# Loading the second token tile of x from ScalarE's queue, and splitting its transposes over four banks, at the start of a SwiGLU feed-forward kernel

## The chip, the core and the metric

The kernel runs on one core of one Trainium2 chip. The metric is the device time of one execution in microseconds (us); lower is better.

## The reference

The function is a SwiGLU feed-forward layer in bf16, with 2048 tokens, model width D = 512 and hidden width F = 1376:

```
B, S, D, F = 1, 2048, 512, 1376
g = _silu(x @ w_gate)
u = x @ w_up
return (g * u) @ w_down
```

## The kernel before

**Tiling.** Tokens are worked in four chunks of 512 (`SC`), hidden features in ten full tiles of 128 and a remainder of 96, and the model width in four slices of 128 (`KD`). TensorE sums over the partition dimension, so both gate and up products need x with its width on the partitions: that is `xT_sb`. A product for one chunk and one feature tile (a "G" group for the gate, a "U" group for up) is four matmuls, one for each width slice, into one PSUM bank. ScalarE applies silu to the G bank, VectorE multiplies the result with the U bank and writes the hidden tile `hT_sb`. The remainder has groups of its own (X and Y). At the end sixteen token tiles ("O" groups) are multiplied with `w_down`, copied out of PSUM and stored.

**Engines and order.** Each engine has its instructions written out in order; they meet through semaphores. The planner lists the groups in the order in which TensorE works them; group number n uses bank n modulo 8 (`NB`), and TensorE takes a bank again after the readers of the group eight places earlier are done (`free`, from the third G or U group on).

**The start.** This is where the change lies. TensorE first runs six matmuls on constants (`N_WARM`, line 290). The first 256 tokens of x come in as they lie in memory, as two token tiles of 128 by 512 (`x0_sb`, loads named t0 and t1, line 101, issued by SyncE). TensorE transposes them by multiplying with an identity (line 297), in four "T" groups: each holds two 128 by 128 transposes in one bank and is copied into `xT_sb` by one copy of 256 columns. The first two width slices of each tile are copied by ScalarE (line 235), the last two by VectorE (line 246). Tokens 256 to 511 come through a transposing load (named x0b, line 76) straight into `xT_sb`.

The first G and the first U group are worked in halves (line 282): G on tokens 0 to 255, U on tokens 0 to 255, then G and U on tokens 256 to 511. In the first halves, the matmul on slice dk waits for the copies that hold slices up to dk; these copies are listed in `x0_ready` with their first slice, engine and place. The second halves wait for x0b. All later groups take 512 tokens at once.

**Loads.** The weights come in slabs of feature tiles, a gate slab and an up slab each: tile 0, tile 1, tiles 2 and 3, tiles 4 to 6, and the rest. In the text wg0 and wu0 are the gate and up slabs of tile 0, wg1 and wu1 those of tile 1, wg2 and wu2 those of tiles 2 and 3. ScalarE issues wg0 and wu0 (line 81), then runs a small silu on constants, ahead of which its function table is loaded (line 224). SyncE issues, in this order, t0, t1, x0b, then wg1, wu1, wg2, wu2 and the rest, the other three chunks of x by transposing loads, and `w_down`.

Of the kernel before, what the change touches and what calls it, by code (L numbers as in the profile page):

```python
# [12 lines left out]
def bass_standalone__swiglu_ffn__prompt_kernel(nc, x, w_gate, w_up, w_down, out):  # L13
    _, S, D = x.shape
    F = w_gate.shape[1]
    P = 128
    KD = D // P
# [5 lines left out]
    TPC = SC // P  # L23
# [8 lines left out]
    xf = x[0]  # L32
# [8 lines left out]
    with ExitStack() as es:  # L41
# [4 lines left out]
        xT_sb = sb("xT_sb", [P, KD, S], BF16)  # L46
# [7 lines left out]
        x0_sb = sb("x0_sb", [P, TPC // 2, D], BF16)  # L54
# [11 lines left out]
        def load_sem(name):  # L66
            loads[name] = sem(f"s_{name}")
            return loads[name]
# [6 lines left out]
        def load_x(eng, name, t0, t1):  # L75
            eng.dma_start_transpose(
                xT_sb[:, :, t0:t1], xf[t0:t1, :]
            ).then_inc(load_sem(name), 16)

        def load_w(eng, name, src, base, f0, f1):  # L80
            eng.dma_start(
                w_sb[:, :, base + f0:base + f1],
                src[:, f0:f1].rearrange("(k p) f -> p k f", p=P),
            ).then_inc(load_sem(name), 16)
# [4 lines left out]
        def load_gate(eng, a, b):  # L89
            load_w(eng, f"wg{a}", w_gate, 0, a * P, min(b * P, F))  # L90

        def load_up(eng, a, b):
            load_w(eng, f"wu{a}", w_up, UPH, a * P, min(b * P, F - 32))

        def loads_on_scalar(act):
            load_gate(act, *slabs[0])
            load_up(act, *slabs[0])

        def loads_on_sync(sp):
            for t in range(TPC // 2):  # L100
                sp.dma_start(x0_sb[:, t, :], xf[t * P:(t + 1) * P, :]).then_inc(load_sem(f"t{t}"), 16)
            load_x(sp, "x0b", HT, SC)
            for a, b in slabs[1:]:
                load_gate(sp, a, b)
                load_up(sp, a, b)
            load_w(sp, "wut", w_up, F - (F - 32), F - 32, F)
            for c in range(1, NSC):
                load_x(sp, f"x{c}", c * SC, (c + 1) * SC)
            sp.dma_start(
                wd_sb[:, 0:NFF, :], w_down[0:NFF * P, :].rearrange("(k p) d -> p k d", p=P)  # L110
            ).then_inc(load_sem("wd"), 16)
            sp.dma_start(wd_sb[0:F_LAST, NFF, :], w_down[NFF * P:F, :]).then_inc(load_sem("wdt"), 16)
# [7 lines left out]
        def add_group(kind, **what):  # L120
            g = dict(kind=kind, at=len(groups), bank=banks[len(groups) % NB], readers=[], **what)
            groups.append(g)
            return g

        def add_op(eng, g, **what):
            n_read[eng] += 1
            op = dict(g=g, at=n_read[eng], **what)
            (act_ops if eng == "A" else dve_ops).append(op)
            g["readers"].append((eng, op["at"]))
            return op  # L130
# [46 lines left out]


        x0_ready = []
        for t in range(TPC // 2):  # L180
            for half, eng in enumerate("AD"):
                g = add_group("T", t=t, k0=2 * half)
                op = add_op(
                    eng, g, kind="copy", stored=(s_I, 0),
                    out=xT_sb[:, 2 * half:2 * half + 2, t * P:(t + 1) * P],
                    src=g["bank"][:, 0:2 * P].rearrange("p (k t) -> p k t", k=2),
                )
                x0_ready.append((2 * half, eng, op["at"]))
        n_T = len(groups)

        for c in range(NSC):
# [7 lines left out]
        for t in range(NST):  # L199
# [3 lines left out]
            for c0, c1 in halves:  # L203
                g = add_group("O", t=t, c0=c0, c1=c1)
                eng = "A" if len(halves) == 2 and c0 == 0 else "D"
                op = add_op(
                    eng, g, kind="copy", out=o_sb[ob][:, c0:c1], src=g["bank"][:, 0:c1 - c0],
                    stored=(s_out[ob], need),
                )
# [4 lines left out]
        def on_sync(sp):  # L214
            loads_on_sync(sp)
            for t, c0, c1, ob, eng, n in stores:
                sp.wait_ge(s_A if eng == "A" else s_D, n)
                sp.dma_start(of[t * P:(t + 1) * P, c0:c1], o_sb[ob][:, c0:c1]).then_inc(s_out[ob], 16)
            for i in range(NOS):
                sp.wait_ge(s_out[i], 16 * n_store[i])  # L220

        def on_scalar(act):
            loads_on_scalar(act)
            act.activation(adummy[:, 0:4], zero_c, ACT.Silu)  # L224
            for op in act_ops:
                act.wait_ge(s_P, op["g"]["at"] + 1)
                if op["kind"] == "silu":
                    if op["free"]:
                        act.wait_ge(s_D, op["free"])
                    fn = ACT.Silu  # L230
                else:
                    if op["stored"][1]:
                        act.wait_ge(*op["stored"])
                    fn = ACT.Copy
                act.activation(op["out"], op["src"], fn).then_inc(s_A, 1)  # L235
# [13 lines left out]
        def on_tensor(pe):  # L249
            landed = set()  # L250

            def need(name):
                if name not in landed:
                    pe.wait_ge(loads[name], 16)
                    landed.add(name)
# [36 lines left out]
            pe.wait_ge(s_I, 1)  # L292
            for g in groups[:n_T]:
                need(f"t{g['t']}")
                for i in range(2):
                    k = g["k0"] + i
                    ins = pe.matmul(  # L297
                        g["bank"][:, i * P:(i + 1) * P], lhsT=x0_sb[:, g["t"], k * P:(k + 1) * P],
                        rhs=ident[:, :], start=True, stop=True,
                    )  # L300
                ins.then_inc(s_P, 1)
# [4 lines left out]
            for g in groups[n_T + 2:]:  # L306
# [27 lines left out]
                else:  # L334
                    t, c0, c1 = g["t"], g["c0"], g["c1"]
# [18 lines left out]
        on_sync(nc.sync)  # L354
        on_scalar(nc.scalar)
        on_tensor(nc.tensor)
        on_vector(nc.vector)

# [27 lines left out]
```

## Time and profile before

| | |
|---|---|
| time, median of 3 runs | 121.23 us (120.81 to 121.36) |
| the profiled execution | 121.29 us, of which the span from first to last instruction is 120.0 us |
| TensorE matmul | 117.0 us busy, 97% of the span |
| VectorE, ScalarE | 44.5 us (37%), 31.1 us (26%) |
| data moved | 8.51 MB, nearly all of the loads in the first fifth of the span |

PE is TensorE's matmuls, PEld its weight loads, DVE VectorE, ACT ScalarE, POOL GpSimd, SP SyncE; a "q" behind an engine's name is its sequencer, which issues the DMAs. Times in the profile count from the first instruction of the program. A duration of a matmul runs from its start to its modelled end; since matmuls overlap, the distance from start to start is what one costs.

### The profile page before, as it was taken

What the parts mean: (1) busy time and instruction counts of PE and PEld (TensorE: products, weight loads), DVE (VectorE), ACT (ScalarE), POOL (GpSimd) and SP (SyncE); (2) the same over time, 40 slices, a digit from 0 to 9 for tenths busy, and PEclk for the clock granted to TensorE, in tenths of its full rate; (3) what the DMA queues carried; (4) which work ended last, traced back from release to release, by engine and by line L of the source; (5) the groups of instructions that cost most, each with busy time, mean ns of one, the idle gap of its engine ahead of it and who ended that gap; (6) DMA issues with size and microseconds to landing.
All of it is one profiled execution on the core that took longest, in us unless ns stands there. A gap on an engine that the chain in (4) does not pass through costs nothing.

```text
span 120.0 us, 1415 instructions
## 1 busy us (share of the span) xinstructions
PE 117.0 (97%) x561; PEld 53.9 (45%) x561; DVE 44.5 (37%) x66; ACT 31.1 (26%) x53; POOL 0.5 (0%) x5
## 2 busy tenths in 40 slices
PE   7899999999999999999999999999999999999993
PEld 2564444444444444444444444344444444444452
DVE  0224433444434444334444334466233224222420
ACT  3333233262333272333262333230000000000001
POOL 1000000000000000000000000000000000000000
DMA  3999999930000000000000000000211121111112
GB/s 89 231 306 372 287 218 182 302 127 0 0 0 0 0 0 5 0 0 5 0 0 0 0 5 0 0 0 0 87 44 44 52 85 44 44 66 66 44 44 87
DMA packets 17254, 8.51 MB, mean 71 GB/s; under 512 B 10496, under 2 KB 17248, under 8 KB 17248
## 3 DMA queue, kind: packets, MB, share of 16 engines
q1 hardware_dynamic: 16192, 8.16, 25.4%
q10 hardware_dynamic: 1056, 0.26, 1.0%
q8 instruction: 4, 0.07, 0.3%
q14 instruction: 2, 0.02, 0.0%
HBM read 4.49 MB, written 2.10 MB: 55 GB/s over the span
## 4 chain that ended last, share of the span: by engine, by line
PE 97%; ACT 0%; DVE 0%; issue 0%
PE bank L282 58%; PE bank L344 32%; PE bank L316 3%; PE bank L290 2%; PE bank L327 2%; PE bank L297 1%; ACT xT_sb L235 0%; DVE o_sb L246 0%
## 5 line engine op out<-in xcount | busy, mean ns | idle before, releaser
L282 PE MATMUL bank<-xT_sb,w_sb 128*128 128x512 bf16 (+1 forms) x328 | 70.2, 376 | 0.4 <-ACT xT_sb L235 0.4
L282 PEld LDWEIGHTS bank<-xT_sb,w_sb 128*128 128x128 bf16 x328 | 32.2, 98 | 37.7 <-issue 0.6
L242 DVE TENSOR_TENSOR hT_sb<-sg_sb,bank 128x512 bf16<-128x512 f32 x40 | 27.5, 688 | 40.8 <-PE bank L282 37.6
L344 PE MATMUL bank<-wd_sb,hT_sb 128*128 128x512 bf16 (+4 forms) x187 | 38.3, 367 | 0.0
L235 ACT ACTIVATE sg_sb<-bank 128x512 f32<-128x512 f32 x40 | 23.8, 596 | 41.6 <-PE bank L282 41.6
L344 PEld LDWEIGHTS bank<-wd_sb,hT_sb 128*128 128x128 bf16 (+1 forms) x187 | 17.8, 98 | 20.7 <-DVE hT_sb L242 0.4
L246 DVE CAST o_sb<-bank 128x512 bf16<-128x512 f32 (+1 forms) x16 | 10.7, 667 | 25.4 <-PE bank L344 25.3
L235 ACT ACTIVATE o_sb<-bank 128x384 bf16<-128x384 f32 x1 | 0.5, 490 | 38.2 <-PE bank L344 38.2
L316 PE MATMUL bank<-xT_sb,w_sb 128*128 128x512 bf16 x16 | 4.1, 379 | 0.0
L242 DVE TENSOR_TENSOR hT_sb<-sgx_sb,bank 32x512 bf16<-32x512 f32 x4 | 2.8, 692 | 3.5 <-ACT sgx_sb L235 3.5
L290 PE MATMUL bank<-const-bfloat16-1.0 128*128 128x512 bf16 x6 | 2.7, 623 | 0.8 <-PEq L371 0.8
L235 ACT ACTIVATE sgx_sb<-bank 32x512 f32<-32x512 f32 x4 | 2.3, 587 | 4.5 <-PE bank L316 4.5
L242 DVE TENSOR_TENSOR hT_sb<-sgy_sb,bank 64x512 bf16<-64x512 f32 x4 | 2.7, 685 | 0.1
L316 PEld LDWEIGHTS bank<-xT_sb,w_sb 128*128 128x128 bf16 x16 | 1.6, 98 | 1.9
L246 DVE CAST xT_sb<-bank 128x256 bf16<-128x256 f32 x2 | 0.8, 424 | 4.2 <-PE bank L297 4.0
L235 ACT ACTIVATE sgy_sb<-bank 64x512 f32<-64x512 f32 x4 | 2.4, 589 | 0.1
L327 PE MATMUL bank<-xT_sb,w_sb 128*64 128x512 bf16 x16 | 1.9, 382 | 0.0
L224 ACT ACT_TABLE_LOAD x1 | 1.3, 1283 | 1.9 <-issue 1.9
L290 PEld LDWEIGHTS bank<-const-bfloat16-1.0 128*128 128x128 bf16 x6 | 0.7, 133 | 1.9 <-issue 1.9
L327 PEld LDWEIGHTS bank<-xT_sb,w_sb 128*64 128x64 bf16 x16 | 0.8, 109 | 1.0 <-DVE hT_sb L242 0.4
L297 PE MATMUL bank<-ident,x_sb 128*128 128x128 bf16 x8 | 1.2, 309 | 0.0
L297 PEld LDWEIGHTS bank<-ident,x_sb 128*128 128x128 bf16 x8 | 0.8, 133 | 0.8 <-issue 0.5
(7 smaller groups left out, 1.7 us busy)
## 6 DMA issues: line engine op xcount, KB each, us to landing
out_dram<-o_sb SPq DMA_DIRECT2D x15, 128.0 KB, 1.7
wd_sb<-in_w_down_dram SPq DMA_DIRECT2D x1, 1280.0 KB, 6.9
w_sb<-in_w_gate_dram SPq DMA_DIRECT2D x1, 480.0 KB, 5.5
w_sb<-in_w_up_dram SPq DMA_DIRECT2D x1, 448.0 KB, 6.1
w_sb<-in_w_gate_dram SPq DMA_DIRECT2D x1, 384.0 KB, 4.6
w_sb<-in_w_up_dram SPq DMA_DIRECT2D x1, 384.0 KB, 5.1
x_sb<-in_x_dram SPq DMA_DIRECT2D x2, 128.0 KB, 2.5
w_sb<-in_w_gate_dram SPq DMA_DIRECT2D x1, 256.0 KB, 3.9
```

The source lines that it names most:

```text
L224: act.activation(adummy[:, 0:4], zero_c, ACT.Silu)
L235: act.activation(op["out"], op["src"], fn).then_inc(s_A, 1)
L242: ins = dve.tensor_tensor(op["out"], op["a"], op["b"], ALU.mult)
L246: ins = dve.tensor_copy(op["out"], op["src"])
L282: ins = pe.matmul(g["bank"][:, n0:n1], lhsT=w_sb[:, dk, col:col + P], rhs=xT_sb[:, dk, c * SC + n0:c * SC + n1], start=(dk == 0), stop=(dk ...
L290: pe.matmul(banks[NB - 1][:, :], lhsT=ones_w, rhs=ones_m, start=True, stop=True)
L297: ins = pe.matmul(g["bank"][:, i * P:(i + 1) * P], lhsT=x0_sb[:, g["t"], k * P:(k + 1) * P], rhs=ident[:, :], start=True, stop=True,)
L316: ins = pe.matmul(g["bank"][:, :], lhsT=w_sb[:, dk, XC0:XC0 + P], rhs=xT_sb[:, dk, c * SC:(c + 1) * SC], start=(dk == 0), stop=(dk == KD - 1),
L327: ins = pe.matmul(g["bank"][y0:y1, :], lhsT=w_sb[:, dk, YC0:YC0 + 64], rhs=xT_sb[:, dk, c * SC:(c + 1) * SC], start=(dk == 0), stop=(dk == ...
L344: ins = pe.matmul(g["bank"][:, 0:c1 - c0], lhsT=hT_sb[0:K, fk, t * P:(t + 1) * P], rhs=wd_sb[0:K, fk, c0:c1], start=(fk == 0), stop=(fk == ...
```

## The change

The load of token tile 1 goes from SyncE to ScalarE, as ScalarE's first load, ahead of wg0 and wu0. So the transposing load x0b becomes SyncE's second load. Tile 0 keeps its two T groups of two transposes each; tile 1 gets four T groups of one transpose each, whose copies of 128 columns go to ScalarE and VectorE in turn (slices 0 and 2 to ScalarE, 1 and 3 to VectorE). There are six T groups in place of four, so every later group has a bank two places on.

```diff
+        def load_t(eng, t):
+            eng.dma_start(x0_sb[:, t, :], xf[t * P:(t + 1) * P, :]).then_inc(load_sem(f"t{t}"), 16)
+
         def loads_on_scalar(act):
+            load_t(act, 1)
             load_gate(act, *slabs[0])
             load_up(act, *slabs[0])
 
         def loads_on_sync(sp):
-            for t in range(TPC // 2):
-                sp.dma_start(x0_sb[:, t, :], xf[t * P:(t + 1) * P, :]).then_inc(load_sem(f"t{t}"), 16)
+            load_t(sp, 0)
             load_x(sp, "x0b", HT, SC)
...
         x0_ready = []
-        for t in range(TPC // 2):
-            for half, eng in enumerate("AD"):
-                g = add_group("T", t=t, k0=2 * half)
+        for t, nk in ((0, 2), (1, 1)):
+            for k0 in range(0, KD, nk):
+                eng = "AD"[(k0 // nk) % 2]
+                g = add_group("T", t=t, k0=k0, nk=nk)
                 op = add_op(
                     eng, g, kind="copy", stored=(s_I, 0),
-                    out=xT_sb[:, 2 * half:2 * half + 2, t * P:(t + 1) * P],
-                    src=g["bank"][:, 0:2 * P].rearrange("p (k t) -> p k t", k=2),
+                    out=xT_sb[:, k0:k0 + nk, t * P:(t + 1) * P],
+                    src=g["bank"][:, 0:nk * P].rearrange("p (k t) -> p k t", k=nk),
                 )
-                x0_ready.append((2 * half, eng, op["at"]))
+                x0_ready.append((k0, eng, op["at"]))
...
             for g in groups[:n_T]:
                 need(f"t{g['t']}")
-                for i in range(2):
+                for i in range(g["nk"]):
```

## Prediction

> **What bounds the kernel now.** I read the chain of waits first, to see whether anything but TensorE sets the end.
>
> ```profile
> 0.84 2.72 PE bank L290 x6
> 3.56 0.80 PE bank L297 x6
> 4.36 0.02 issue
> 4.38 0.39 ACT xT_sb L235
> 4.77 0.14 issue
> 4.91 17.95 PE bank L282 x88
> ```
>
> From 4.91 us on the chain is TensorE without a break up to the last copy; nothing after that is touched by the change except bank numbers, which keep their distance of eight. So all that can be won lies ahead of 4.91, plus what a late load can add shortly behind it. The last link before the G group is ScalarE's copy of tile 1, with 0.14 us from its end to the first G matmul.
>
> Next the timeline of 3.3 to 5.0 us, for what that copy waited for.
>
> ```profile
> 3.81 0.38 ACT L235 ACTIVATE xT_sb<-bank 128x256 bf16<-128x256 f32 x1 [0.45 <-PE bank L297]
> 3.94 0.34 PEld L297 LDWEIGHTS bank<-ident,x_sb 128*128 128x128 bf16 x4 [0.23 <-DMA x_sb<-in_x_dram]
> 4.02 1.00 DVE L246 CAST xT_sb<-bank 128x256 bf16<-128x256 f32 x2 [4.02 <-PE bank L297]
> 4.38 0.38 ACT L235 ACTIVATE xT_sb<-bank 128x256 bf16<-128x256 f32 x1 [0.19 <-PE bank L297]
> ```
>
> TensorE waited 0.23 us for t1 (it landed at 3.90), ScalarE then 0.19 us for tile 1's transposes. The copies are short, but the two engines have two each, in a row.
>
> Then the busy time by stretches, for TensorE's speed and the load on the DMA engines:
>
> ```profile
> core 0: us, PE busy (x) PEld busy (x) DVE busy (x) ACT busy (x) POOL busy (x), PEclk, DMA share, GB/s
> 2.00:3.00 1.00, 1.00 (x4) 0.29 (x2) 0.00 (x0) 1.00 (x1) 0.00 (x0) 1.00 0.93 250
> 5.00:6.00 1.00, 1.00 (x6) 0.63 (x6) 0.02 (x1) 0.00 (x0) 0.00 (x0) 1.00 1.09 194
> 6.00:7.00 1.00, 1.00 (x11) 0.90 (x10) 0.00 (x0) 0.09 (x1) 0.00 (x0) 1.00 0.94 214
> ```
>
> All matmuls in the last two rows have 256 columns at most, and the count nearly doubles. In the records of single matmuls the start-to-start distance of the 256-column matmuls is 0.213 us up to 5.92 and 0.109 us from 6.06 on; the one between, 0.133, puts the switch to the full rate at about 5.98. (The PEclk column shows 1.00 throughout; the distances do not.) By 5.98 the G/U work has done 5.25 matmuls. The DMA engines are full from 2.0 us on, so a load that goes sooner pushes another back.
>
> Last, the issue-to-landing times of the loads:
>
> ```profile
> x_sb<-in_x_dram SPq DMA_DIRECT2D x2, 128.0 KB, 2.5
> w_sb<-in_w_gate_dram ACTq DMA_DIRECT2D x1, 128.0 KB, 2.7
> w_sb<-in_w_up_dram ACTq DMA_DIRECT2D x1, 128.0 KB, 3.6
> xT_sb<-in_x_dram SPq DMA_TRANSPOSE x1, 4.1
> ```
>
> With the issue times this gives landings at 3.07 (t0), 3.52 (wg0), 3.90 (t1), 4.94 (wu0), 5.84 (x0b), then 6.39, 7.39 and 8.14 (wg1, wu1, wg2). They follow one another; no two land together.
>
> **The change, part by part.** *The issues.* ScalarE's queue gets one more issue, 0.40 us by SP's rows for t0 and t1 (0.398 and 0.411), plus some 0.03 of gap. wg0 is issued at 1.23 instead of 0.80, wu0 at 1.73 instead of 1.29. Behind them the table load (1.28 us) starts at 2.29 instead of 1.85, and the small silu (0.20) ends at 3.79 instead of 3.35. ScalarE's first copy started at 3.81 after a wait of 0.45: this wait is the cover, and it is used up to 0.02 us. If ScalarE's issues take 0.53 each, as its second did, the first copy is some 0.1 late. SyncE loses one issue: x0b and all its later loads are issued 0.46 earlier, which wins nothing by itself as the DMA engines are full.
>
> *t1's landing.* Not in the trace from ScalarE's queue. Best case: as t0, issue plus 2.27, 3.07. Worst: where t1 lands now, 3.90. I take wg0's row, the first load of that queue: issue plus 2.7, 3.5. Needed at about 3.75, so TensorE's wait for t1 goes, and its eight transposes run from 3.35 to 4.20 at 0.107 each, instead of to 4.35.
>
> *The copies.* ScalarE's 256- and 512-column operations take 383 and 597 ns, so 128 columns take about 276 (an estimate on the same line); VectorE's 424 and 667 give 303. Each engine has one copy of 256 and two of 128: ScalarE 0.94 us instead of 0.77, VectorE 1.03 instead of 0.85. That is 0.17 to 0.18 more work each, on the path, against finer waits. From ScalarE's first copy (3.81 to 4.19): slice 0 of tile 1 is ready at 4.49, slice 2 at 4.80. VectorE (first copy 4.02 to 4.45): slice 1 at 4.78, slice 3 at 5.11. Each start of a matmul comes 0.145 after the copy it waits for, as now (4.761 to 4.906). So G on slice 0 starts at 4.64, on slice 1 at max(4.64 + 0.213, 4.78 + 0.145) = 4.93, slice 2 at 5.14, slice 3 at 5.35 (5.11 + 0.145 is sooner), and U at 5.56. Before, U started at 5.71. The two added waits of TensorE have only the four G matmuls behind them. Gain: 0.15 us at the slow rate.
>
> *What that is worth.* If the switch to the full rate stays at 5.98, the 0.15 us holds 0.7 of a slow matmul, which would have cost 0.109 each later: 0.07 to 0.08 us. If the switch moves with the start, 0.15. I take 0.10.
>
> The Trainium skill has a rule that bears on this, "TensorE: Matmul & The Clock Gate", Part 1 (The HAM clock gate): the full clock comes after about 3.4 us of a free-running window with enough activity, so an earlier start would only move work into the slow time. By that rule the sum would be the 0.07; no row of one profile shows whether the switch is tied to the clock or to the work.
>
> *The loads behind.* wg0 now is second on its queue. If it takes t1's present place, it lands at 3.90; needed at 4.6, cover 0.7. wu0, third, between its present 4.94 and x0b's 5.84 (by then all five first loads are through whatever their order); needed at 5.45, which is 0.11 ahead of its matmul. I take 5.2, nearer to the present row, since x0b's transfer cannot start before its own issue of 1.3 us is well under way (now 3.81 in the packet records, 2.08 after its issue began; by that 3.35 after the change). x0b stays at about 5.84, needed at 6.1 instead of 6.28: cover 0.2. wg1, wu1, wg2 have 0.66, 0.52 and 0.63 us to their matmuls (by the single records), more than the 0.15 that TensorE gains. All this hides.
>
> A second rule speaks against the change: "DMA: Bandwidth & Descriptors", section "Issuing engines are not separate DMA queues", says that loads from several engines run on the same 16 DMA engines and interleave, so a second queue only saves issue time. By it t1's gain is taken from t0 and wg0; this is the first rival below, with the landings above as its measure.
>
> **Sum.** 121.29 (profiled) - 0.10 = 121.19. The profiled execution lies 0.06 above the median of the runs: 121.1.
>
> **The rivals.** *t0 is passed by t1.* The two equal loads are issued within 0.01 us of each other, and t0 has no head start any more. Landings are 0.38 to 0.44 apart now; if t1 goes first, t0 lands at about 3.47, and the transposes start at 3.62 instead of 3.35. Everything up to U moves by 0.27: U at 5.83, 0.12 later than now, 0.06 us lost in all: 121.3. For it: the same engines, equal shapes. Against it: in the present profile SP's load did land first though both queues started together.
>
> *The full rate comes sooner,* since TensorE's pause at 3.8 for t1 goes. At most all eight first-half matmuls run at 0.109, but x0b, at 5.84, then holds the second halves until about 5.98 instead of 6.28: 0.30 gained, 120.9. Beyond this the weights would bind: wu1 allows 0.52. So no case on these rows gains much over 0.5 us, and a clear gain of over 0.6 is nearly shut out.
>
> *Slower: wu0 lands late.* It is third on ScalarE's queue, and shares the DMA engines with x0b's and then wg1's packets, which now start sooner. From a landing of 5.6 on U starts later than now. At x0b's row (5.84) U starts at 5.95, which costs 0.14 to 0.24. If it is pushed to where wg1 lands now, 6.39, U starts at 6.5; 1.25 matmuls that were done by 5.98 come at the full rate after it: 0.52 + 0.14 = 0.66, 121.9. Against it: the two queues' packets alternate about evenly when both are waiting (packet records, 3.0 to 3.3 us), and wu0 has half of x0b's bytes.
>
> **How the numbers follow.** 0.5% is 0.6 us, about what a measurement of this kernel can tell from no change (three runs spread over 0.55). Forecast: 0.50 (121.0 to 121.3). t0 passed: 0.18. Sooner full rate: 0.12. wu0 late: 0.15, of it 0.1 far enough to cost over 0.6. The last 0.05 is a later full rate after new pauses of TensorE, which would cost half of the delay. Faster by over 0.5%: 0.12, from runs that come out low in the first and third case; within: 0.66; slower: 0.22, the late wu0, the late full rate and runs that come out high. The range takes the first three cases with 0.3 us of spread of the runs on both sides, and half of the fourth: 120.5 to 121.8.
>
> **What would show it.** Right: t1 lands before 3.75 and no PEld wait on x_sb between the transposes; ScalarE's 128-column copies at 0.28 us; the first G matmul at 4.6 to 4.7, and U at 5.5 to 5.6; the chain of waits unbroken after it. Wrong: the first transpose later than 3.4 (t0 passed); a PE wait on a w_sb or xT_sb load behind 4.6 us (a load late); the 0.109 distance starting far from 5.98; or any difference after 24 us.

## The result, and the profile after

The changed kernel takes 121.84 us (median of ten runs, 121.49 to 123.57); the kernel before, run beside it, 121.16 (120.81 to 121.62). The ratio is 1.0047, with a 95% interval of 1.0029 to 1.0066: slower by about half a per cent. Two of the ten runs came in a slower state (123.42 and 123.57) and are left out of the ratio. The profiled execution took 121.81 us, its span is 120.5 instead of 120.0.

The chain of waits of the changed kernel (start, length, what):

```profile
1.71 0.03 issue
1.74 4.57 DMA w_sb<-in_w_up_dram
6.31 0.05 issue
6.35 17.02 PE bank L286 x84
23.38 0.86 PE bank L320 x4
24.24 17.27 PE bank L286 x80
```

Where ScalarE's copy of tile 1 stood, there is a load: wu0, issued at 1.74 and landed at 6.31. The chain is unbroken from 6.35 on, and from here it runs 0.52 us behind the kernel before (second chunk at 24.24 instead of 23.72). So the whole loss is made before 6.35.

The timeline from 3.3 us on:

```profile
3.55 0.78 PEld L301 LDWEIGHTS bank<-ident,x_sb 128*128 128x128 bf16 x8 [0.90 <-issue]
3.58 1.01 PE L301 MATMUL bank<-ident,x_sb 128*128 128x128 bf16 x8
3.99 0.81 ACT L239 ACTIVATE xT_sb<-bank 128x256 bf16<-128x256 f32 x3 [0.20 <-PE bank L301]
4.20 0.82 DVE L250 CAST xT_sb<-bank 128x256 bf16<-128x256 f32 x3 [4.20 <-PE bank L301]
4.73 0.65 PE L286 MATMUL bank<-xT_sb,w_sb 128*128 128x256 bf16 x4
6.35 1.38 PE L286 MATMUL bank<-xT_sb,w_sb 128*128 128x256 bf16 x11 [0.97 <-DMA w_sb<-in_w_up_dram]
```

The pause between the transposes of tile 0 and tile 1 is gone (eight in one piece), but they start at 3.58 instead of 3.35. G still starts sooner, at 4.73 instead of 4.91. Then four matmuls, and an idle time of 0.97 us before U.

The busy time by stretches:

```profile
5.00:6.00 1.00, 0.38 (x4) 0.10 (x1) 0.02 (x1) 0.00 (x0) 0.00 (x0) 1.00 1.33 248
6.00:7.00 1.00, 0.65 (x6) 0.59 (x7) 0.00 (x0) 0.00 (x0) 0.00 (x0) 1.00 1.18 308
```

TensorE is idle for most of a microsecond while the DMA engines move more than they did in this stretch before (248 GB/s against 194): not too few bytes, but other ones than those it waits for.

The issues, with the time to landing last:

```profile
x_sb<-in_x_dram ACTq DMA_DIRECT2D x1, 128.0 KB, 2.8
x_sb<-in_x_dram SPq DMA_DIRECT2D x1, 128.0 KB, 2.6
w_sb<-in_w_gate_dram ACTq DMA_DIRECT2D x1, 128.0 KB, 3.1
w_sb<-in_w_up_dram ACTq DMA_DIRECT2D x1, 128.0 KB, 4.6
xT_sb<-in_x_dram SPq DMA_TRANSPOSE x1, 5.1
```

Each takes longer than before: t0 2.6 (2.3), wg0 3.1 (2.7), wu0 4.6 (3.6), x0b 5.1 (4.1). Only t1 gains, by its earlier issue.

### The profile page after: what moved, and what is told of

It reads as the page before. It is cut to its first block, busy times and chain, and to the rows that moved or that the text cites. A ratio compares the mean times of both kernels' runs of the same rounds, so it can differ in the third digit from the quotient of the medians.

```text
span 120.5 us, 1416 instructions
## 1 busy us (share of the span) xinstructions
PE 116.7 (97%) x561; PEld 53.5 (44%) x561; DVE 44.5 (37%) x67; ACT 31.1 (26%) x54; POOL 0.5 (0%) x5
## 4 chain that ended last, share of the span: by engine, by line
PE 93%; DMA 4%; ACTq 1%; DVE 0%; issue 0%
PE bank L286 57%; PE bank L348 32%; DMA w_sb<-in_w_up_dram 4%; PE bank L320 3%; PE bank L331 2%; ACTq L81 0%; ACTq L96 0%; DVE o_sb L250 0%
## 5 line engine op out<-in xcount | busy, mean ns | idle before, releaser
L250 DVE CAST xT_sb<-bank 128x128 bf16<-128x128 f32 (+1 forms) x3 | 0.8, 328 | 4.2 <-PE bank L301 4.2
```

The source lines that it names most:

```text
L250: ins = dve.tensor_copy(op["out"], op["src"])
```

## The experiments

All ratios are against the kernel before, run on the same chip. First, each half of the change alone.

**The finer copies alone** (split_only): t1 back on SyncE.

```diff
         def loads_on_scalar(act):
-            load_t(act, 1)
...
             load_t(sp, 0)
+            load_t(sp, 1)
```

> Only the finer copies of tile 1; all loads as in the kernel before. Theory (the late wu0 behind the transposing load is the whole loss): t1 lands at 3.9, wu0 at about 4.9, no wait of TensorE on wu0; ratio to the kernel before 0.998 to 1.001. Rival (the added copies cost): G's first matmul after 4.95, and ratio above 1.002.

0.9996 (0.9976 to 1.0016). TensorE did not wait for wu0 (landed 4.53), but in this execution, where the full rate came before the first G matmul, for x0b:

```profile
4.67 4.68 PE L286 MATMUL bank<-xT_sb,w_sb 128*128 128x256 bf16 x27 [0.29 <-ACT xT_sb L239]
5.75 2.28 PEld L286 LDWEIGHTS bank<-xT_sb,w_sb 128*128 128x128 bf16 x16 [0.33 <-DMA xT_sb<-in_x_dram]
```

G starts at 4.67, and the copies cost nothing; what they win is lost again at x0b, which landed at 5.71.

**The loads alone** (loads_only): tile 1 with two transposes to a bank, as before.

```diff
-        for t, nk in ((0, 2), (1, 1)):
+        for t, nk in ((0, 2), (1, 2)):
```

> Only the moved loads; tile 1 keeps two T groups of two transposes and copies of 256 columns. Theory: wu0 lands at 6.2 to 6.4 and the first U matmul starts at about 6.35, as in the changed kernel; ratio to the kernel before 1.004 to 1.005, since the copies' gain is lost in that wait. Rival (the copies cost): ratio nearer to 1.001.

1.0043 (1.0022 to 1.0063); wu0 landed at 6.25 and U started at 6.29. The chain is that of the changed kernel:

```profile
1.73 4.52 DMA w_sb<-in_w_up_dram
6.25 0.05 issue
6.29 17.02 PE bank L286 x84
```

So the loss belongs to the moved loads, and the copies make no difference that can be measured.

**wu0 as SyncE's second load** (wu0_on_sync):

```diff
         def loads_on_scalar(act):
             load_t(act, 1)
             load_gate(act, *slabs[0])
-            load_up(act, *slabs[0])
...
             load_t(sp, 0)
+            load_up(sp, *slabs[0])
             load_x(sp, "x0b", HT, SC)
```

> The changed kernel with one load more moved: wu0 is SyncE's second load, ahead of the transposing load x0b; ScalarE issues t1 and wg0 only. Theory: wu0 lands by 5.0, x0b at about 5.9 to 6.2, TensorE does not wait for wu0, first U matmul at 5.2 to 5.5; ratio 0.996 to 1.000. Rival (the five first loads are late as a whole, whatever their order, since the DMA engines lose time when two queues mix): x0b or wu0 still lands at 6.3, ratio 1.002 to 1.005.

1.0013 (0.9995 to 1.0032), just above what was expected. wu0 landed at 4.20, x0b at 5.90, and the wait for wu0 is gone:

```profile
4.84 1.93 PE L286 MATMUL bank<-xT_sb,w_sb 128*128 128x256 bf16 x14
5.94 0.55 PEld L286 LDWEIGHTS bank<-xT_sb,w_sb 128*128 128x128 bf16 x6 [0.21 <-DMA xT_sb<-in_x_dram]
```

U started at 5.41. With wu0 out of the way the loss is no longer to be told from zero. What remains is t0 landing at 3.56 and wg0 at 4.67: no gain either.

**x0b as plain loads** (plain_x0b). Two loads of 128 tokens, untransposed, in runs of 256 bytes; tokens 256 to 511 are therefore not transposed.

```diff
-            load_x(sp, "x0b", HT, SC)
+            for a, name in enumerate(("x0b", "x0c")):
+                t0 = HT + a * P
+                sp.dma_start(
+                    xT_sb[:, :, t0:t0 + P], xf[t0:t0 + P, :].rearrange("p (k f) -> p k f", f=P)
+                ).then_inc(load_sem(name), 16)
...
+                    need("x0c")
```

> The changed kernel with x0b as two plain loads of 512 runs of 256 bytes each, as many bytes and runs as the transposing load, which leaves tokens 256 to 511 untransposed. Theory (a transposing load takes most turns from the other queue): wu0 lands at 5.0 to 5.4 and TensorE waits for it by 0.3 at most; ratio 0.996 to 1.001. Rival (third place on ScalarE's queue beside any load of SyncE): wu0 still lands after 6.0, ratio 1.003 to 1.006.

wu0 landed at 6.01, still after 6.0, and the idle time before U was 0.68 us; the ratio is 1.0016 (0.9998 to 1.0034), below what the rival gave. My theory of the transposing load as the cause is refuted: with plain loads wu0 came 0.3 us sooner in this one execution, of a delay of 1.4 (6.31 against 4.94).

**x0b held back by 0.6 us** (hold_x0b): SyncE waits for the second constant matmul.

```diff
             load_t(sp, 0)
+            sp.wait_ge(s_H, 1)
             load_x(sp, "x0b", HT, SC)
...
+                if i == 1:
+                    warm.then_inc(s_H, 1)
```

> The changed kernel, with SyncE waiting for the second constant matmul (its end is at about 1.85 us) before it issues x0b; so x0b is issued at about 1.9 us instead of 1.26, close to its 1.73 in the kernel before. Theory (wu0 is late because x0b, issued before it, takes most turns of the DMA engines while both wait): wu0 lands at 5.0 to 5.5, TensorE waits for it by at most 0.3, x0b lands at 6.1 to 6.5; ratio to the kernel before 0.999 to 1.003. Rival (third place on ScalarE's queue is enough): wu0 lands after 5.9, ratio 1.004 to 1.006.

Neither: wu0 landed at 5.82, x0b at 6.64, and TensorE waited for both; 1.0071 (1.0042 to 1.01). By the packets in the trace, x0b's first came at 3.68, when ScalarE's queue had moved 297 KB, 41 more than t1 and wg0 hold; from 4.5 to 5.0 the two queues moved 35 KB together, where the kernel before moved 120. Being issued 0.15 ahead of x0b does not help wu0. My next theory was that what counts is whether their transfers fall together.

**wu0 issued later in the kernel before** (late_wu0): loads and copies as before, but ScalarE waits for the second constant matmul between wg0 and wu0.

```diff
             load_gate(act, *slabs[0])
+            act.wait_ge(s_H, 1)
             load_up(act, *slabs[0])
...
+                if i == 1:
+                    warm.then_inc(s_H, 1)
```

> The kernel before, with ScalarE waiting for the second constant matmul before it issues wu0: at about 1.9 us instead of 1.29, behind x0b's issue at 1.73; t0, t1, wg0 and the copies as before; the table load and the small silu move with it, so ScalarE's first copy is some 0.15 late. Theory (behind x0b, wu0 loses the turns): wu0 lands at 5.6 to 6.3 though it is second on its queue, U starts at 5.8 to 6.4; ratio 1.002 to 1.006. Rival (third place on its queue): wu0 lands at about 5.2 to 5.5, no wait, ratio 1.000 to 1.002.

wu0 landed at 6.10, second on its queue; U at 6.15; 1.0035 (1.0015 to 1.0056). x0b, whose issue had not changed, landed at 6.90 instead of 5.84. A delay of 0.59 us in the issue of wu0 alone brings most of the loss, and both transfers suffer. It is x0b that holds the chain of this run:

```profile
1.72 5.18 DMA xT_sb<-in_x_dram
```

**x0b held back further** (hold_long): as hold_x0b, with the fifth constant matmul. It was meant to keep x0b's transfer away from wu0's; all later loads of SyncE wait with it.

```diff
-                if i == 1:
+                if i == 4:
                     warm.then_inc(s_H, 1)
```

> The changed kernel with x0b held until the fifth constant matmul (its end is at about 3.13 us), so that x0b's packets start near 5.1 us. wu0 stays third on ScalarE's queue, issued at 1.73. Theory now (wu0 and x0b both land late whenever their transfers fall together; either alone is quick): wu0 lands at 4.5 to 5.0 and U starts by 5.5; x0b lands at 7.0 to 7.4 and TensorE waits for it by 1 us or more; ratio 1.008 to 1.015. Rival (third place on its queue makes wu0 late): wu0 lands after 5.7 though nothing of x0b is moving.

wu0 landed at 5.39, between the two; x0b took 3.3 us instead of 5.1 and landed at 6.51, sooner than expected; 1.0066 (1.0042 to 1.0091). The issues:

```profile
w_sb<-in_w_up_dram ACTq DMA_DIRECT2D x1, 128.0 KB, 3.7
xT_sb<-in_x_dram SPq DMA_TRANSPOSE x1, 3.3
```

The ratio is not wu0's, since the chain of this run goes through wg1, which was held with x0b and landed at 7.65:

```profile
3.16 1.32 SPq L77
4.48 0.06 issue
4.54 3.11 DMA w_sb<-in_w_gate_dram
7.65 0.05 issue
```

Against the changed kernel, x0b and every load behind it on SyncE's queue go out 1.9 us later, and wu0 lands at 5.39 instead of 6.31. So 0.9 us of its landing goes with what SyncE issues; whether it is x0b or the loads behind it, this run can't tell. Nor did it keep the transfers apart: x0b's first packet came at 4.56, when 63 of wu0's 128 KB were still to go, and these had gone by 4.94. Packets of x0b beside wu0 are thus not enough to make it slow, and my theory fails in this form. And wu0, issued at 1.73, takes 3.7 us, about the 3.6 of the first profile before, from an issue 0.44 later. The stretches of this run (PE busy, clock, DMA share, GB/s) show its slow part:

```profile
3.50:4.50 1.00, 0.97 (x9) 1.00 0.48 54
4.50:5.50 1.00, 0.82 (x5) 1.00 1.11 252
```

From 3.5 to 4.5 only ScalarE's queue moved data, nearly all of it wu0's, at 54 GB/s; the kernel before moved 225 in that microsecond. wu0's issue had ended at 2.26. What ran beside it was SyncE's issue of x0b, 3.16 to 4.48; but in the kernel before the same issue ran from 1.73 to 3.03, and 250 GB/s were moved from 2.0 to 3.0. Why wu0 was slow is open.

**A try for a faster version** (one_queue): t0, t1, wu0 and x0b from SyncE in this order, wg0 alone from ScalarE, with the finer copies.

```diff
         def loads_on_scalar(act):
-            load_t(act, 1)
             load_gate(act, *slabs[0])
-            load_up(act, *slabs[0])
...
             load_t(sp, 0)
+            load_t(sp, 1)
+            load_up(sp, *slabs[0])
             load_x(sp, "x0b", HT, SC)
```

> A try for a faster version: the finer copies stay; SyncE issues t0, t1, wu0, x0b in this order and ScalarE wg0 alone, so wu0 and x0b are in one queue, one behind the other, and t0 has its head start. Theory: t0 lands at 3.1, t1 at 3.9, wu0 at 4.4 to 4.9, x0b at 5.9 to 6.3 (its issue is 0.5 later than in the kernel before); no long wait; ratio 0.999 to 1.002, so no clear gain, since x0b holds the second halves. If x0b's landing does not follow its issue, 0.996 to 0.999.

1.0039 (1.0022 to 1.0056), worse than expected. t0 (2.95) and G (4.55) are the earliest of all profiles and t1 (3.71) is earlier than before, but wu0, again issued at 1.72, landed at 5.28, and x0b, issued 0.46 later than before, at 6.36, and holds the chain:

```profile
2.19 4.17 DMA xT_sb<-in_x_dram
6.36 0.05 issue
6.41 5.15 PE bank L286 x27
```

**The two kernels once more** (before_again, after_again).

> The kernel before once more, for a second look at where TensorE goes over to the full rate. If it is tied to the program, the 256-column matmuls go from 0.213 to 0.109 us at about 6.0 again; if it is not, at another time between 4.1 and 6 us, as over the four kernels so far. With an early one, x0b at about 5.85 holds the second halves.

> The changed kernel once more, for a second look at the landings. wu0 at 6.2 to 6.4, t0 at 3.4 to 3.5, U at 6.25 to 6.45; the full rate from any time between 4.1 and 6 us, without effect on U's start.

The changed kernel repeated itself: 121.78 us, wu0 at 6.27, U at 6.31, and t0 a little sooner, at 3.32. The kernel before did not: 120.79 us, with 256-column matmuls 0.109 apart from the start, but for one wait for a copy. The stretch in which the first profile had six matmuls:

```profile
5.00:6.00 1.00, 1.00 (x11) 0.81 (x10) 0.00 (x0) 0.00 (x0) 0.00 (x0) 1.00 0.79 154
```

So the moment of the full rate is not tied to the program. The two executions of the kernel before differ by 0.5 us; x0b landed sooner as well (5.52 against 5.84), so how much of it is the rate is not shown. In the changed kernel it seems worth nothing, since TensorE waits for wu0 in any case: the profile of loads_only, with matmuls of G still 0.21 apart, took 121.78, and so did that of after_again, where they were 0.109 apart by 5.1.

The landings side by side, from the issue records (us):

| kernel | wu0 issued | wu0 landed | x0b issued | x0b landed |
|---|---|---|---|---|
| before (two profiles) | 1.29 | 4.94, 4.42 | 1.73, 1.72 | 5.84, 5.52 |
| split_only | 1.29 | 4.53 | 1.73 | 5.71 |
| wu0_on_sync | 1.26 | 4.20 | 1.72 | 5.90 |
| hold_long | 1.73 | 5.39 | 3.16 | 6.51 |
| one_queue | 1.72 | 5.28 | 2.19 | 6.36 |
| after (two profiles) | 1.74, 1.73 | 6.31, 6.27 | 1.26, 1.27 | 6.37, 6.37 |
| loads_only | 1.73 | 6.25 | 1.25 | 6.17 |
| plain_x0b (two loads for x0b) | 1.73 | 6.01 | 1.26, 1.97 | 4.95, 6.21 |
| hold_x0b | 1.73 | 5.82 | 1.88 | 6.64 |
| late_wu0 | 1.89 | 6.10 | 1.72 | 6.90 |

Issued by 1.3, wu0 lands by 4.94. Issued at 1.72 or later, it lands at 5.28 or later, on either queue. Of these later ones, hold_long and one_queue, with x0b issued after 2.1, are late by about the issue of wu0 alone: 3.6 to 3.7 us from issue to landing, as in the first profile before. In the others, with x0b issued between 1.25 and 1.9, wu0 lands 0.4 to 0.9 later than in hold_long. So there are two parts of the delay, each from few executions; what makes the second is not shown.

## Why the prediction was wrong

**What bounds the kernel** held: everything is decided ahead of the first full groups, and the chain behind is unchanged.

**The step that failed is wu0's landing.** It was put at 5.2, with 5.84 as the upper end, on the ground that by then all five first loads are through whatever their order. They were not: wu0 landed at 6.31 and x0b at 6.37. Two supports broke. First, the even alternation of the queues, read off t1 and wg0 (80 packets to 86 from 3.0 to 3.3 us), does not hold for wu0 beside x0b: from 4.0 to 4.5 us the trace of the changed kernel has 93 KB of SyncE's queue and 14 KB of ScalarE's, all in packets of 256 bytes. Second, the bound took the total as kept, while wg1, behind x0b in SyncE's queue, moved bytes before wu0 was done: when wu0's last data packet went, at 5.42, SyncE's queue had moved 420 KB, 36 more than t0 and x0b hold. And 0.9 us passed from then to its landing, where the kernel before took 0.6. The cover of 0.25 us, taken as enough, was gone. In its place the runs show two parts: with its issue 0.44 later, wu0 landed at 5.39 instead of 4.94 when SyncE's loads were held back (hold_long), and at 6.31 when they were not. Why the second part arises stays open.

**The rival was right in place and price.** "wu0 lands late" gave 121.9 for a landing at 6.39; the time is 121.84 for one at 6.31. Its working, put to U's start of 6.35, gives (6.35 - 5.98) + 1.25 x 0.109 = 0.51; the first 512-column matmul started 0.525 later than before (7.674 against 7.149). For the time from landing to matmul it took 0.11, where 0.05 was measured. There is luck in so close a match: it sets two single executions side by side, and the kernel before took 0.5 us less in another. The fault was its chance, 0.15. The row that should have raised it was x0b's own in the profile before: its packets began at 3.81, when wu0 had 37 of its 128 KB to go. The change delayed wu0's issue by 0.44 and put x0b's 0.47 ahead, so that x0b's packets began at 3.16, when ScalarE's queue had 204 of its 384 KB to go.

**t0 passed by t1** came half true: t0 still landed first, but at 3.44, 0.37 later, and the transposes started 0.23 later, at 3.58. The rule of the Trainium skill ("DMA: Bandwidth & Descriptors", section "Issuing engines are not separate DMA queues") that loads from several engines interleave on the same DMA engines agrees with this: t1's 0.28 was paid by t0 (0.37) and wg0 (0.83). Of wg0's 0.83, 0.45 is its later issue.

**The copies** were sized well singly (277 ns for 276 on ScalarE, 280 for 303 on VectorE), but not as a sum: an engine's next copy begins before the last one ends, so ScalarE's three took 0.81 and not 0.94. G at 4.73 against the forecast 4.64 is t0's delay less this. VectorE's 303 rested on 667 ns for 512 columns, the mean of a group that holds a copy of 128 columns too; the 512-column copies alone took 692, which gives 290. Their gain was forecast as too small to measure, and none was measured (0.9996).

**The full rate** did come sooner, by about 4.9. The changed kernel was not its cause, as before_again shows; and the profile that I worked from was one of a late full rate, so what I read off it as slack is smaller in other executions.

## What to carry to other kernels

A load moved to another queue delays every load behind it there and advances every one behind its old place; look which loads then go out side by side, and do not bound their landings by the total of bytes. Slack at the start of a kernel should be read from more than one execution where the engine's rate there varies. Here the better place for t1 was worth less than the place it took from wu0.

## What the runs showed of the hardware that was not expected

- With the issue of wu0 0.59 later and that of x0b as before (late_wu0), both landed over a microsecond later: 6.10 and 6.90, against 4.94 and 5.84.
- A load of 128 KB issued at 1.73 behind two others of its queue moved at 54 GB/s from 3.5 to 4.5 us, with no data of another queue beside it (hold_long); in the kernel before, issued at 1.29 behind one, its queue moved 93 KB in the half microsecond from 3.5 to 4.0.
- The change to the full matmul rate came at 5.98 us in one execution of the kernel before and ahead of 4.9 in another, with 0.5 us between their times, in which x0b's earlier landing has a part that was not measured.
